# FNet mixing and a ReGLU feed-forward: feature tiles taken in pairs, two PSUM banks to one VectorE instruction

## The chip, the cores and the metric

The kernel runs on one core of one Trainium2 chip. The metric is the device time of one execution in microseconds. The kernel before takes 650.49 us, the median of three runs (649.2 to 650.72).

Engine names in the profile: PE is TensorE's matmul, PEld its weight load, DVE is VectorE, ACT is ScalarE, POOL is GpSimd, SP is the engine whose queue issues most transfers. PSUM is the memory in which these kernels place the tiles that PE writes; a tile of 128 x 512 fp32 in it is called a bank here. The granted clock is the share of its full clock that TensorE was given. L505 is line 505 of the kernel that the line belongs to. The two kernels have different line numbers.

## The reference

```python
# x: 8 x 3008 x 256, w_gate and w_val: 256 x 1536, w_out: 1536 x 256, all fp32
X = np.fft.fft(np.fft.fft(x, axis=1), axis=2).real      # FNet mixing
x = X.reshape(8 * 3008, 256)
gate = np.maximum(x @ w_gate, 0.0)
val = x @ w_val
out = (gate * val) @ w_out                               # 24064 x 256, fp32
```

## The kernel before

Each batch is transformed into tiles `pq` of 128 x 2 x 512 (bf16), three blocks of columns to a batch. The feed-forward then runs as 288 steps: 8 batches, 3 blocks, NF = 12 tiles of 128 features. The spectrum of a real input is symmetric, so one step serves 512 rows and their mirrored rows. With the two halves pq0 and pq1 and the weights wc, ws and wm (wm is -2 ws):

- gate: G = wc·pq0 + ws·pq1, and ScalarE takes its Relu, `gs`. Then G += wm·pq1 gives the mirrored gate, and ScalarE takes its Relu, `gm`.
- value: V = wc·pq0. VectorE makes E = nb·af + V from it (called the even below). Then V += ws·pq1, and VectorE takes the direct product h0 = gs·V.
- mirrored value: VectorE makes E = 2E - V (the reflection, L519), and GpSimd makes the mirrored product h1 = gm·E with its columns reversed (L511).
- unsplit (relief) steps skip the even and the reflection: PE makes the mirrored value by a third matmul, V += wm·pq1, and VectorE multiplies it (from step 216 on GpSimd does, from a copy that ScalarE makes). These are the first 18 steps, then every sixth up to step 48, then every twelfth.

The output matmuls of step t-12 (8 of 256 columns in each step) fill the gaps. GpSimd also folds the input rows of a later batch: `fold` is a generator, and the loop takes one piece from it in each step. The rows for it are asked for at step `tl` of a batch, and its first piece is emitted at step `tf`.

```python
def split(t):
    return 18 <= t < len(steps) and t % (6 if t < 48 else 12) != 5

def value(t, part):
    ...                                                  # cut
    if part == 0:
        e["V"] = psv.tile([128, 512], F32, tag="v", name="V")      # one bank, three of them
        nc.tensor.matmul(e["V"][:], lhsT=wc[1][:, fs], rhs=pq[:, 0, :], start=True, stop=split(t))
    else:
        nc.tensor.matmul(e["V"][:], lhsT=ws[1][:, fs], rhs=pq[:, 1, :], start=False, stop=True, ...)
        nc.vector.tensor_tensor(e["h"][:, 0, :], e["gs"][:], e["V"][:], op=ALU.mult)

def mirror_value(t):
    ...                                                  # cut
    if split(t):
        nc.vector.scalar_tensor_tensor(e["E"][:, cols], e["E"][:, cols], 2.0, e["V"][:, cols],
                                       op0=ALU.mult, op1=ALU.subtract)
        mirror_h(t, nc.gpsimd, e["E"])
    else:
        nc.tensor.matmul(e["V"][:, cols], lhsT=wm[1][...], rhs=pqt[b, blk][:, 1, cols], ...)
        ...                                              # cut

plan = {0: (18, 24, ...), 1: (7, 13, ...), 2: (7, 13, ...)}      # (tl, tf, steps of the transform)

for t in range(n + NF):
    if 0 < t <= n:
        mirror_gate(t - 1)
    if t < n:
        gate(t)
    if 0 < t <= n:
        if split(t - 1):
            value(t - 1, 1)
        else:
            mirror_value(t - 1)
    if t < n and not split(t):
        value(t, 0)
        value(t, 1)
    for fn in extra.get(t, ()):                          # loads, transform of the next batch
        fn()
    if t >= NF:
        out_piece(t - NF, 0)
    if split(t):
        value(t, 0)
        even(t)
    if t >= NF:
        out_piece(t - NF, 1)
    if 0 < t <= n and split(t - 1):
        mirror_value(t - 1)
    while folds and next(folds[0], folds) is folds:      # one piece of fold, at the end of the step
        folds.pop(0)
```

Of the kernel before, what the change touches and what calls it, by code (L numbers as in the profile page):

```python
# [43 lines left out]
def kernel(ctx: ExitStack, tc, x, w_gate, w_val, w_out, out):  # L44
# [12 lines left out]
    HB = 2 * NF + 1  # L57
# [5 lines left out]
    psd = ctx.enter_context(tc.tile_pool(name="psd", bufs=1, space=PS))  # L63
    psg = ctx.enter_context(tc.tile_pool(name="psg", bufs=2, space=PS))
    psv = ctx.enter_context(tc.tile_pool(name="psv", bufs=3, space=PS))
    pso = ctx.enter_context(tc.tile_pool(name="pso", bufs=2, space=PS))
# [76 lines left out]
    def bank(b, name):  # L143

        if b == 0:
            return psv.tile([128, 512], F32, tag="v", name=name)
        return psd.tile([128, 512], F32, tag="d", name=name)
# [3 lines left out]
    def stage1(b, c, evac):  # L151
# [4 lines left out]
        ps = bank(b, "ps1")  # L156
# [34 lines left out]
    def rotate(b):  # L191
        t4 = t4t[b]
        ps = bank(b, "psr")
        nc.tensor.matmul(ps[:, 0:NKA], lhsT=rot[:], rhs=t4[:, :, H], start=True, stop=True)
        nc.vector.tensor_copy(t4[:, :, H], ps[:, 0:NKA])
# [3 lines left out]
    def stage2(b, blk, cs, evac):  # L199
# [4 lines left out]
        ps = bank(b, "ps2")  # L204
        for g in range(4):
            nc.tensor.matmul(ps[:, g * 128:(g + 1) * 128], lhsT=t4[:, 4 * blk + g, cs * H:(cs + 1) * H],  # L206
                             rhs=m2[:, cs, :], start=True, stop=True)
        if evac == "act":
            nc.scalar.copy(pq[:, cs, :], ps[:])
        else:  # L210
            nc.vector.tensor_copy(pq[:, cs, :], ps[:])  # L211
# [26 lines left out]
    cd = None  # L238
    for n in range(DF // 512):
        if n == 2:  # L240
            cd = hp.tile([128, 2, H], F32, tag="h", name="cd")
        for i in range(2):
            for c in range(3):
                wst[i, n, c] = hp.tile([128, 512], F32, tag="h", name="wst")

    def load_w(n, which=(0, 1)):
        for i in which:
            w = (w_gate, w_val)[i]
            for c in range(2):
                nc.sync.dma_start(out=wst[i, n, c][:], in_=w[c * 128:(c + 1) * 128, n * 512:(n + 1) * 512])  # L250

    def pair_w(n, i, eng):

        lo, hi, up = (wst[i, n, c] for c in range(3))
        eng.tensor_tensor(up[:], lo[:], hi[:], op=ALU.add)
        eng.tensor_tensor(lo[:], lo[:], hi[:], op=ALU.subtract)

    def fold_w(n, i, cs, evac="act"):

        ps = (pso.tile([128, 512], F32, tag="o", name="psw") if i == 0 or n else  # L260
              psg.tile([128, 512], F32, tag="g", name="psw"))
        for k, w in ((0, wst[i, n, 2]), (1, wst[i, n, 0])):
            nc.tensor.matmul(ps[64 * k:64 * k + 64, :], lhsT=cd[:, cs, 64 * k:64 * k + 64], rhs=w[:],  # L263
                             start=True, stop=True)
# [8 lines left out]
    def nyquist():  # L273

        ps = psd.tile([128, 512], F32, tag="d", name="psn")
# [8 lines left out]
    with tc.tile_pool(name="sp", bufs=1, space=SB) as sp:  # L284
# [32 lines left out]
        ps = psd.tile([128, 512], F32, tag="d", name="psk")  # L317
# [67 lines left out]
        pl.iota(kbi[:], pattern=[[0, 4], [1, NB]], base=0, channel_multiplier=0, allow_small_or_imprecise_dtypes=True)  # L385
# [66 lines left out]
    ep = ctx.enter_context(tc.tile_pool(name="ep", bufs=4, space=SB))  # L452
# [3 lines left out]
    ht = {}  # L456

    def mirrored(t):

        blk = steps[t][1]  # L460
        return slice(NB if blk == 0 else 0, 512 - NB if blk == NBLK - 1 else 512)

    def split(t):

        return 18 <= t < len(steps) and t % (6 if t < 48 else 12) != 5

    def gate(t):
        b, blk, f = steps[t]
        pq, fs = pqt[b, blk], slice(f * 128, (f + 1) * 128)
        e = ht[t] = {"h": hp.tile([128, 2, 512], BF16, tag="h", name="h"),  # L470
                     "G": psg.tile([128, 512], F32, tag="g", name="G"),
                     "gs": gp.tile([128, 512], F32, tag="gs", name="gs")}
        nc.tensor.matmul(e["G"][:], lhsT=wc[0][:, fs], rhs=pq[:, 0, :], start=True, stop=False)  # L473
        nc.tensor.matmul(e["G"][:], lhsT=ws[0][:, fs], rhs=pq[:, 1, :], start=False, stop=True)  # L474
        nc.scalar.activation(e["gs"][:], e["G"][:], ACTF.Relu)  # L475
        cols = mirrored(t)
        if cols.stop - cols.start < 512:

            lo = 0 if cols.start else cols.stop
            nc.gpsimd.memset(e["h"][:, 1, lo:lo + NB], 0.0)  # L480

    def mirror_gate(t):
        b, blk, f = steps[t]
        e, cols = ht[t], mirrored(t)
        nc.tensor.matmul(e["G"][:, cols], lhsT=wm[0][:, f * 128:(f + 1) * 128], rhs=pqt[b, blk][:, 1, cols],  # L485
                         start=False, stop=True, skip_group_check=True)
        e["gm"] = ep.tile([128, 512], F32, tag="gm", name="gm")
        nc.scalar.activation(e["gm"][:, cols], e["G"][:, cols], ACTF.Relu)  # L488

    def value(t, part):  # L490
        b, blk, f = steps[t]
        e, pq, fs = ht[t], pqt[b, blk], slice(f * 128, (f + 1) * 128)
        if part == 0:
            e["V"] = psv.tile([128, 512], F32, tag="v", name="V")
            nc.tensor.matmul(e["V"][:], lhsT=wc[1][:, fs], rhs=pq[:, 0, :], start=True, stop=split(t))  # L495
        else:
            nc.tensor.matmul(e["V"][:], lhsT=ws[1][:, fs], rhs=pq[:, 1, :], start=False, stop=True,  # L497
                             skip_group_check=split(t))
            nc.vector.tensor_tensor(e["h"][:, 0, :], e["gs"][:], e["V"][:], op=ALU.mult)  # L499

    def even(t):
        b, blk, f = steps[t]
        e, cols = ht[t], mirrored(t)
        e["E"] = ep.tile([128, 512], F32, tag="e", name="E")
        nc.vector.scalar_tensor_tensor(e["E"][:, cols], nbt[b, blk][:, cols], af[:, f:f + 1], e["V"][:, cols],  # L505
                                       op0=ALU.mult, op1=ALU.add)

    def mirror_h(t, eng, val):

        e, cols = ht[t], mirrored(t)  # L510
        eng.tensor_tensor(free(e["h"][:], 512 + cols.start + NB - 1, [NB, (cols.stop - cols.start) // NB], [-1, NB]),  # L511
                          e["gm"][:, cols].rearrange("p (a k) -> p a k", k=NB),
                          val[:, cols].rearrange("p (a k) -> p a k", k=NB), op=ALU.mult)

    def mirror_value(t):
        b, blk, f = steps[t]
        e, cols = ht[t], mirrored(t)
        if split(t):
            nc.vector.scalar_tensor_tensor(e["E"][:, cols], e["E"][:, cols], 2.0, e["V"][:, cols],  # L519
                                           op0=ALU.mult, op1=ALU.subtract)  # L520
            mirror_h(t, nc.gpsimd, e["E"])
        else:
            nc.tensor.matmul(e["V"][:, cols], lhsT=wm[1][:, f * 128:(f + 1) * 128], rhs=pqt[b, blk][:, 1, cols],  # L523
                             start=False, stop=True, skip_group_check=True)
            if t < 6 * NBLK * NF:
                mirror_h(t, nc.vector, e["V"])
            else:
                e["E"] = ep.tile([128, 512], F32, tag="e", name="E")
                nc.scalar.copy(e["E"][:, cols], e["V"][:, cols])
                mirror_h(t, nc.gpsimd, e["E"])  # L530
# [3 lines left out]
    def out_piece(t, half):  # L534

        b, blk, f = steps[t]
        for k in range(8 * f + 4 * half, 8 * f + 4 * half + 4):
            gi, ff = divmod(k, NF)
            sg, s = divmod(gi, 4)
            g = 3 - s if sg else s  # L540
            if s == 0 and ff == 0:
                state["os"] = op.tile([128, 4, D], F32, tag="os", name="os")
            if s % 2 == 0 and ff == 0:
                state["po"] = pso.tile([128, 2, D], F32, tag="o", name="po")
            po, os_ = state["po"], state["os"]
            nc.tensor.matmul(po[:, s % 2, :], lhsT=ht[t - f + ff]["h"][:, sg, g * 128:(g + 1) * 128],  # L546
# [3 lines left out]
            if t - f == len(steps) - NF and sg == 1:  # L550
                nc.vector.tensor_copy(os_[:, s:s + 1, :], po[:, s % 2:s % 2 + 1, :])  # L551
                store_last(b, blk, os_, s)
                continue
            if s % 2 == 1:
                nc.scalar.copy(os_[:, s - 1:s + 1, :], po[:])  # L555
            if s == 3:
                store(b, blk, sg, os_)

    def store_last(b, blk, os_, s):

        for u in range(4):
            ka = NKA * u + 4 * blk
            if s == 0 and ka + 3 == 47:
                continue
            (nc.sync if u % 2 or s < 2 else nc.scalar).dma_start(
                out=view(out, (b * S + NA - ka - 3 + s) * D, [[NA * D, NB], [1, D]]), in_=os_[32 * u:32 * u + 32, s, :])

    def store(b, blk, sg, os_):
        for u in range(4):
            ka = NKA * u + 4 * blk  # L570
            src = os_[32 * u:32 * u + 32].rearrange("p g d -> p (g d)")
            if sg == 0:
                nc.sync.dma_start(out=view(out, (b * S + ka) * D, [[NA * D, NB], [1, 4 * D]]), in_=src)
                continue

            lo = 1 if ka + 3 == 47 else 0
            hi = 3 if ka == 0 else 4
            row = b * S + NA - ka - 3 + lo
            nc.sync.dma_start(out=view(out, row * D, [[NA * D, NB], [1, (hi - lo) * D]]),
                              in_=src[:, lo * D:hi * D])  # L580
# [89 lines left out]
```

## Time and profile before

| what | before | view |
|---|---|---|
| span of the profiled run | 648.3 us | page, head |
| PE busy from 300 to 400 us | 99% | windows |
| VectorE, GpSimd busy in the same stretch | 92%, 91% | windows |
| 36 steps (one batch) in the middle | 73.8 us | timeline, between gate Relus |
| GpSimd's waits for rows before `fold`, each batch | 1.4 to 3.0 us | timeline of GpSimd |

The page's first part has the busy time of each engine, as a share of the span, and the number of its instructions:

```profile
PE 626.1 (97%) x4170; PEld 408.8 (63%) x4246; DVE 565.0 (87%) x889; ACT 425.1 (66%) x813; POOL 508.1 (78%) x716
```

The windows view, for 300 to 400 us. After the length come the busy times of PE, PEld, DVE, ACT and POOL with their instructions, then the granted clock, the DMA share and GB/s:

```profile
300.00:400.00 100.00, 99.14 (x687) 66.52 (x699) 92.16 (x145) 68.59 (x132) 90.54 (x126) 1.00 0.45 111
```

PE has no gap worth a name in the middle of the kernel, at the full clock. VectorE and GpSimd are close behind it. Their times show in the timeline. Its columns are the start, the duration, the engine, the line, the operation, the tiles and their shapes; a bracket at the end, where there is one, gives the engine's idle time just before and who ended it. PE first, then VectorE in the same stretch:

```profile
311.97 0.38 PE L485 MATMUL G<-pq,wm 128*128 128x512 bf16 x1
312.19 0.38 PE L473 MATMUL G<-pq,wc 128*128 128x512 bf16 x1
312.40 0.38 PE L474 MATMUL G<-pq,ws 128*128 128x512 bf16 x1
```

```profile
311.15 0.69 DVE L499 TENSOR_TENSOR h<-gs,V 128x512 bf16<-128x512 f32 x1
311.81 0.75 DVE L505 SCALAR_TENSOR_TENSOR E<-nb,af,V 128x512 f32<-128x512 bf16 x1
312.47 0.68 DVE L519 SCALAR_TENSOR_TENSOR E<-E,V 128x512 f32<-128x512 f32 x1
313.11 0.69 DVE L499 TENSOR_TENSOR h<-gs,V 128x512 bf16<-128x512 f32 x1
```

A record of 0.38 us isn't PE's cost of a matmul: the next one starts 0.215 us later. VectorE's three instructions start 0.65 us apart and come round in 1.96 us.

### The profile page before, as it was taken

The page shows a single profiled execution, that of the slowest core. Times are in us where ns is not written, and L with a number is a line of the kernel's source. Part 1 is how long each engine was busy: PE and PEld are TensorE (multiplying, and loading weights), DVE is VectorE, ACT ScalarE, POOL GpSimd, SP SyncE. Part 2 cuts the span into 40 slices and gives each one's busy share as a digit, 9 for nine tenths or more (in the row PEclk, how much of TensorE's full clock was granted, in tenths as well). Part 3 has the DMA queues.
Part 4 walks back from the last instruction along what each step waited for, and adds up shares of the span by engine and source line. Part 5 has one row for each costly group of instructions (what it writes and reads, how often), then busy time and mean ns, then how long its engine had stood idle before and what let it go on. Part 6 is the DMA issues. An engine that isn't in the chain of part 4 may idle for free.

```text
span 648.3 us, 12804 instructions
## 1 busy us (share of the span) xinstructions
PE 626.1 (97%) x4170; PEld 408.8 (63%) x4246; DVE 565.0 (87%) x889; ACT 425.1 (66%) x813; POOL 508.1 (78%) x716
## 2 busy tenths in 40 slices
PE   7888999999999999999999999999999999999995
PEld 3424666666666666666666666666666666666664
DVE  8857688889898998989989998989988988989991
ACT  5465676776766667677676666676666766766660
POOL 9648669967998799968998699967998666666660
PEclk9699999999999999999999999999999999999999
DMA  9792483295125551195334752285312142112113
GB/s 234 241 234 46 104 215 85 69 208 168 40 82 120 143 161 45 47 199 146 81 74 115 165 148 55 50 177 152 96 50 73 31 131 73 50 34 64 32 41 88
DMA packets 32823, 70.77 MB, mean 109 GB/s; under 512 B 4650, under 2 KB 22146, under 8 KB 30754
## 3 DMA queue, kind: packets, MB, share of 16 engines
q1 hardware_dynamic: 30228, 58.03, 33.9%
q0 software_dynamic: 2336, 11.80, 8.7%
q8 instruction: 33, 0.54, 0.4%
q14 instruction: 34, 0.28, 0.1%
q10 hardware_dynamic: 192, 0.13, 0.1%
HBM read 39.77 MB, written 30.96 MB: 109 GB/s over the span
## 4 chain that ended last, share of the span: by engine, by line
PE 89%; DVE 6%; issue 2%; DMA 2%; ACT 1%; SPq 0%; DVEq 0%; ACTq 0%
PE po L546 38%; PE V L497 10%; PE G L474 9%; PE G L485 9%; PE V L495 8%; PE G L473 8%; PE ps L164 2%; PE ps L206 2%; DVE E L505 2%; DVE h L499 1%; PE V L523 1%; PE psw L263 1%; DMA xl<-in_x_dram 1%; DVE eo L136 1%; DVE eo L132 1%
## 5 line engine op out<-in xcount | busy, mean ns | idle before, releaser
L511 POOL TENSOR_TENSOR h<-gm,E 128x480 bf16<-128x480 f32 (+1 forms) x251 | 307.7, 1226 | 90.9 <-DVE E L519 63.9
L546 PE MATMUL po<-wo,h 128*128 128x256 bf16 x2304 | 337.1, 272 | 2.8 <-DVE os L551 1.1
L546 PEld LDWEIGHTS <-h 128*128 128x128 bf16 x2304 | 222.7, 98 | 91.1 <-issue 3.4
L488 ACT ACTIVATE gm<-G 128x480 f32<-128x480 f32 (+1 forms) x288 | 167.4, 581 | 126.8 <-PE G L485 118.7
L499 DVE TENSOR_TENSOR h<-gs,V 128x512 bf16<-128x512 f32 x288 | 195.7, 687 | 17.6 <-ACT gm L488 11.5
L505 DVE SCALAR_TENSOR_TENSOR E<-nb,af,V 128x480 f32<-128x480 bf16 (+1 forms) x245 | 177.6, 725 | 23.3 <-PE V L495 12.6
L475 ACT ACTIVATE gs<-G 128x512 f32<-128x512 f32 x288 | 171.8, 597 | 0.8 <-PE G L474 0.8
L519 DVE SCALAR_TENSOR_TENSOR E<-E,V 128x480 f32<-128x480 f32 (+1 forms) x245 | 161.2, 658 | 0.0
L497 PE MATMUL V<-pq,ws 128*128 128x512 bf16 x287 | 108.7, 379 | 2.2 <-DVE E L505 1.7
L485 PE MATMUL G<-pq,wm 128*128 128x480 bf16 (+1 forms) x288 | 106.7, 370 | 2.2 <-ACT gs L475 2.2
L474 PE MATMUL G<-pq,ws 128*128 128x512 bf16 x281 | 106.5, 379 | 2.2 <-DVE pq L211 0.4
L495 PE MATMUL V<-pq,wc 128*128 128x512 bf16 x255 | 96.6, 379 | 0.0
L473 PE MATMUL G<-pq,wc 128*128 128x512 bf16 x253 | 95.9, 379 | 0.1
L555 ACT COPY os<-po 128x512 f32<-128x512 f32 x94 | 55.0, 585 | 60.2 <-PE po L546 60.2
L104 POOL TENSOR_TENSOR eo<-xl 94x254 bf16<-94x254 f32 (+2 forms) x100 | 74.6, 750 | 0.4
L101 POOL TENSOR_TENSOR xl<-xl,xh 94x510 f32<-94x510 f32 (+2 forms) x50 | 65.9, 1319 | 3.9
L497 PEld LDWEIGHTS <-ws 128*128 128x128 bf16 x288 | 28.2, 98 | 33.7
L474 PEld LDWEIGHTS <-ws 128*128 128x128 bf16 x288 | 28.2, 98 | 31.5 <-issue 0.2
L511 DVE TENSOR_TENSOR h<-gm,V 128x480 bf16<-128x480 f32 (+1 forms) x37 | 24.6, 665 | 22.7 <-ACT gm L488 17.1
L174 ACT CAST t<-ps 96x512 bf16<-96x512 f32 x63 | 36.9, 586 | 5.7 <-PE ps L162 5.2
L495 PEld LDWEIGHTS <-wc 128*128 128x128 bf16 x288 | 28.1, 98 | 11.0 <-issue 4.3
L485 PEld LDWEIGHTS <-wm 128*128 128x128 bf16 x288 | 28.2, 98 | 7.6 <-issue 4.1
(108 smaller groups left out, 348.1 us busy)
## 6 DMA issues: line engine op xcount, KB each, us to landing
out_dram<-os SPq DMA_DIRECT2D x173, 128.0 KB
xl<-in_x_dram SPq DMA_DIRECT2D x7, 1360.0 KB
Td<-t SPq DMA_DIRECT2D x7, 768.0 KB
t<-Td SPq DMA_DIRECT2D x7, 768.0 KB
nb<-Nd SPq DMA_DIRECT2D x24, 128.0 KB
xl<-in_x_dram SPq DMA_DIRECT2D x7, 238.0 KB
xl<-in_x_dram SPq DMA_DIRECT2D x4, 384.0 KB
xh<-in_x_dram SPq DMA_DIRECT2D x4, 384.0 KB
```

The costliest lines, as they stand in the source:

```text
L473: nc.tensor.matmul(e["G"][:], lhsT=wc[0][:, fs], rhs=pq[:, 0, :], start=True, stop=False)
L474: nc.tensor.matmul(e["G"][:], lhsT=ws[0][:, fs], rhs=pq[:, 1, :], start=False, stop=True)
L475: nc.scalar.activation(e["gs"][:], e["G"][:], ACTF.Relu)
L485: nc.tensor.matmul(e["G"][:, cols], lhsT=wm[0][:, f * 128:(f + 1) * 128], rhs=pqt[b, blk][:, 1, cols], start=False, stop=True, skip_group_ ...
L488: nc.scalar.activation(e["gm"][:, cols], e["G"][:, cols], ACTF.Relu)
L495: nc.tensor.matmul(e["V"][:], lhsT=wc[1][:, fs], rhs=pq[:, 0, :], start=True, stop=split(t))
L497: nc.tensor.matmul(e["V"][:], lhsT=ws[1][:, fs], rhs=pq[:, 1, :], start=False, stop=True, skip_group_check=split(t))
L499: nc.vector.tensor_tensor(e["h"][:, 0, :], e["gs"][:], e["V"][:], op=ALU.mult)
L505: nc.vector.scalar_tensor_tensor(e["E"][:, cols], nbt[b, blk][:, cols], af[:, f:f + 1], e["V"][:, cols], op0=ALU.mult, op1=ALU.add)
L511: eng.tensor_tensor(free(e["h"][:], 512 + cols.start + NB - 1, [NB, (cols.stop - cols.start) // NB], [-1, NB]), e["gm"][:, cols].rearrange ...
L519: nc.vector.scalar_tensor_tensor(e["E"][:, cols], e["E"][:, cols], 2.0, e["V"][:, cols], op0=ALU.mult, op1=ALU.subtract)
L546: nc.tensor.matmul(po[:, s % 2, :], lhsT=ht[t - f + ff]["h"][:, sg, g * 128:(g + 1) * 128], rhs=wo[:, ff, :], start=(ff == 0), stop=(ff == ...
```

## The change

The intent: VectorE pays its fixed cost (about 0.11 us an instruction by the prediction's estimate) once for two steps, so that it no longer needs the relief steps and their extra matmul. Steps run in pairs. The pair's V, E, gs, gm and h are tiles of two banks or two halves; product and reflection cover both in one instruction; the two evens stay single. PSUM is divided anew: two V pairs of two banks (before: three single banks), no bank kept for the transform, which borrows the output bank that is idle. The column blocks shift by 16, so that the mirrored part is 496 or 512 columns wide and the direct one 496, 512 or 497. VectorE's copy of the rotation goes to ScalarE. Some pieces of the next batch's transform move by one or two steps in the plan. E and gm have three pair buffers (before: four single ones).

The core of the diff. The new output code, the row lists for the stores, the banks of the first transform and the removed lines of the old loop are cut.

```diff
-    psd = ctx.enter_context(tc.tile_pool(name="psd", bufs=1, space=PS))
-    psv = ctx.enter_context(tc.tile_pool(name="psv", bufs=3, space=PS))
-    pso = ctx.enter_context(tc.tile_pool(name="pso", bufs=2, space=PS))
+    psv = ctx.enter_context(tc.tile_pool(name="psv", bufs=2, space=PS))
+    pso = ctx.enter_context(tc.tile_pool(name="pso", bufs=1, space=PS))
...
+    def borrow(name):
+        return pso.tile([128, 512], F32, tag=f"o{(turn['o'] + 1) % 2}", name=name)
...
-    ep = ctx.enter_context(tc.tile_pool(name="ep", bufs=4, space=SB))
+    ep = ctx.enter_context(tc.tile_pool(name="ep", bufs=3, space=SB))
...
     def split(t):
-        return 18 <= t < len(steps) and t % (6 if t < 48 else 12) != 5
+        return t >= NF
...
+    def direct_h(p):
+        t = 2 * p
+        ds = direct(t)
+        nc.vector.tensor_tensor(pair(t, "h")[:, :, 0, 0:ds.stop - ds.start], pair(t, "gs")[:, :, ds],
+                                pair(t, "V")[:, :, ds], op=ALU.mult)
...
+            nc.vector.scalar_tensor_tensor(E[:, :, cols], E[:, :, cols], 2.0, V[:, :, cols],
                                            op0=ALU.mult, op1=ALU.subtract)
+            mirror_h(p, nc.gpsimd, E)
...
+    def between(t):
         for fn in extra.get(t, ()):
             fn()
         while folds and next(folds[0], folds) is folds:
             folds.pop(0)
+    for p in range(n + NF // 2):
+        t = 2 * p
+        live = p < n
+        if 0 < p <= n:
+            mirror_gate(t - 1)
+        if live:
+            gate(t)
+            value(t, 0)
+            if not split(t):
+                value(t, 1)
+        fill(t, 0)
+        between(t)
+        if live:
+            value(t + 1, 0)
+            if not split(t):
+                value(t + 1, 1)
+        if 0 < p <= n:
+            (direct_h if split(t - 1) else mirror_value)(p - 1)
+        if live:
+            if split(t):
+                even(t)
+                even(t + 1)
+        fill(t, 1)
+        if live:
+            mirror_gate(t)
+            gate(t + 1)
+            if not split(t):
+                direct_h(p)
+        fill(t + 1, 0)
+        between(t + 1)
+        if 0 < p <= n and split(t - 1):
+            mirror_value(p - 1)
+        if live:
+            for k in range(2):
+                value(t + k, 1 if split(t) else 2)
+        fill(t + 1, 1)
```

## The prediction

> What bounds it now. From step 48 on, TensorE. The windows of 200 to 500 us show PE busy 99%, and a batch of 36 steps, read in the timeline between the gate's first Relus (step 72 at 190.14 us, step 108 at 263.90), takes 73.8 us. The timeline spaces 512-column matmuls by 215 ns, 480 by 202, 256 by 108; 36 steps of about 4587 columns, three relief matmuls and the next batch's transform add up to the same 73.8. So PE has no gap there. VectorE is as full in unrelieved steps: its three instructions start 0.65 us apart, 1.94 us per step, PE's step too. The page's 687 ns includes a tail that overlaps the next start; the fixed part is about 0.11 us.
>
> What changes from step 12 on.
> - PE: direct blocks shrink to 496/512/497 columns, mirrored ones go from 480/512/480 to 496/512/496: about 31 columns, 13 ns, less per step: 276 steps, 3.5 us.
> - The 31 relief steps lose their 202-215 ns matmul: 6.4 us.
> - VectorE per pair: product 1003/0.96+0.11 = 1.16 us, reflection 1.16, two evens 1.27: 3.6 us against PE's 3.86. It was 3.9. Slack, no time by itself.
> - GpSimd: about 2.3 us per pair instead of 2.4; 192 memsets of 0.12 us vanish.
> - ScalarE takes the rotation: small.
> So a steady batch should be 72.7 us; steps 36 to 72 gain 3.7, 12 to 36 2.6, the last batch 1.6 us. In the tail, two PE waits of 0.5 us on the last output copies go, as each group has its own bank. About 15 us in all.
>
> What it costs.
> - The first 12 steps are unsplit. Today they overlap step by step (26.1 us between the Relus of steps 0 and 12). In pairs they become a loop: second gate, ScalarE's two Relus (0.45 us apart), one product of 1.2 us over both banks, then the mirrored value matmuls, the next pair. I add up 4.5 us per pair without weight folding against 3.05 now; folds and copies in even steps lie in the chain too: about 33 us. Cost 7 us.
> - The fold of batch 2 (three-row pieces, about 1.35 us per step) with 1.15 us of reflections gives GpSimd 2.5 us per step against PE's 2.0, from step 24 to 41. Without relief it falls behind by 5-7 us; the three E buffers cover about 3. Cost 2-3 us, once.
> - Output blocks of 112 or 113 columns: [...] The trace agrees that 96-column loads are slower, 123 ns against 98, though matmuls behind them kept 108 ns spacing. 384 such matmuls; I count 0-2 us.
>
> Sum: 650.5 - 15 + 7 + 2.5 + 1 = 646; I think some head losses overstated and say 644 us, range 635 to 652. Chances: faster over 2% 0.13, within 2% 0.83, slower 0.04. The gain is capped because the relieved engine was tied with PE, not above it.
>
> Signs. Right: 36 steps at 72.7 us in the middle; VectorE waiting on PE at its evens; no third value matmul after step 12; steps 0 to 12 about 33 us, with PE waiting on VectorE's product. Wrong: middle batches of 74 us or more, PE waiting on VectorE, on ScalarE's output copy (borrowed bank) or on GpSimd; or a head of 26 us.
>
> What would make it wrong: two-bank VectorE reads slower per column than one-bank ones; 112-column loads not hidden (up to 5 us); GpSimd's lag stalling every batch; a head better overlapped than I think (then 637).

650.5 - 15 + 7 + 2.5 + 1 comes to 646, from which the prediction goes to 644. The 1 us for the narrower output blocks is an estimate: in the trace before, the 105 loads of 96 columns of L164 have a mean of 124 ns, those of 128 columns one of 98.

## More of the kernel before

L99 is the first instruction of a piece of `fold`, and it waits for the rows to land, six times in all, for 11.5 us. Here is one such wait, with the issue of the load on SP's queue and then GpSimd's timeline:

```profile
277.87 0.82 SPq L83 DMA_DIRECT2D xl<-in_x_dram  x2
```

```profile
295.97 0.22 POOL L99 TENSOR_TENSOR eo<-xl,xh 94x4 bf16<-94x4 f32 x1 [1.92 <-DMA xh<-in_x_dram,ix]
...
297.49 1.27 POOL L511 TENSOR_TENSOR h<-gm,E 128x512 bf16<-128x512 f32 x1
```

The fold goes on 18.1 us after SP asked for the rows. What it waited for last are the rows of `xh`, which GpSimd had asked for itself at 277.49 us. GpSimd stands still for 1.92 us, then mixes pieces of `fold` and mirrored products, and nobody waits for it long enough to hold up PE.

The summary of waits gives, for each pair of waiting line and releaser, the total, the count and the longest. Two lines of GpSimd's:

```profile
POOL eo L99 <- DMA xh<-in_x_dram,ix: 9.3, 5, 3.0
POOL eo L99 <- DMA xl<-in_x_dram: 2.2, 1, 2.2
```

## The result, and the profile after

| | median of runs | lowest to highest | runs |
|---|---|---|---|
| before, same rounds | 650.61 us | 649.2 to 651.59 | 4 |
| after | 691.69 us | 689.94 to 693.12 | 4 |

The ratio is 1.0632, with a 95% interval of 1.0598 to 1.0666: the change costs 6.3%. Ratios here are the mean time of one kernel's runs over the mean of the other's of the same rounds, so they aren't quite the ratio of the medians quoted beside them. The result is correct. It lies far outside the predicted range of 635 to 652 us.

Where the 42.9 us between the two profiled spans came from, read in the timeline from the start of the gate's first Relu at each step:

| stretch | before | after | difference | predicted |
|---|---|---|---|---|
| start, to step 0 | 35.51 | 38.51 | +3.0 | 0 |
| steps 0 to 12 | 26.11 | 34.90 | +8.8 | +7 |
| steps 12 to 36 | 52.15 | 56.99 | +4.8 | -2.6 |
| steps 36 to 72 | 76.37 | 81.53 | +5.2 | -3.7 + 2.5 |
| steps 72 to 216, four batches with a fold | 295.90 | 313.79 | +17.9 | -1.1 each |
| steps 216 to 252, a batch without a fold | 73.84 | 74.76 | +0.9 | -1.1 |
| steps 252 to 276 | 47.62 | 49.23 | +1.6 | about -1.1 |
| step 276 to the end | 40.8 | 41.5 | +0.7 | about -1.5 |

The table already holds a hint. There are eight batches, and rows are folded two batches ahead, so the seventh (from step 216) has no fold in it. It takes 74.76 us where the four before it take 78.4 on average. So two things are wrong in the steady part: about 3.7 us a batch that come with the fold, and about 2 us a batch, against the predicted 72.7, that don't.

The page after, its first part and GpSimd's row of busy tenths in 40 slices:

```profile
PE 636.6 (92%) x4200; PEld 414.0 (60%) x4231; DVE 548.6 (79%) x630; ACT 432.7 (63%) x846; POOL 512.6 (74%) x412
...
POOL 9539458995999589975999579974999555555552
```

VectorE's instructions went from 889 to 630 and its busy time fell by 16 us, as intended. It bought nothing: PE's share fell from 97% to 92%. GpSimd is busy 74% in all, but its row swings between 4 or 5 tenths and 9 in a steady beat, one swing for each batch. The windows view of 300 to 400 us shows the same loss; PE was at 99.14 there:

```profile
300.00:400.00 100.00, 96.02 (x656) 64.61 (x660) 83.84 (x94) 68.77 (x136) 75.93 (x60) 1.00 0.52 124
```

The waits after (the line numbers are those of the new kernel: L98 is the old L99, L538 the old L511, L525 the even, L546 the reflection, L518 the value matmuls, L531 the direct product):

```profile
DVE E L525 <- PE V L518: 47.7, 82, 2.6
DVE E L525 <- POOL h L538: 42.3, 32, 4.1
POOL eo L98 <- DMA xl<-in_x_dram: 26.4, 4, 7.0
POOL eo L98 <- DMA xh<-in_x_dram,ix: 23.4, 3, 10.5
...
PE V L518 <- DVE E L525: 22.0, 18, 3.7
...
PE V L518 <- DVE h L531: 10.5, 6, 2.5
```

Of the waits for rows, 10.5 us are one wait in the start, which is not new: the traces of the kernel before and of its two variants below have it too, at 10.6 to 11.1 us. Read from the bottom up, these lines are a chain. PE waits for VectorE's evens; the evens wait for GpSimd's mirrored products; and GpSimd waits for rows. One instance, in the order of cause. SP asks for the rows, and GpSimd waits for them:

```profile
305.47 0.78 SPq L82 DMA_DIRECT2D xl<-in_x_dram  x2
```

```profile
323.04 0.22 POOL L98 TENSOR_TENSOR eo<-xl,xh 94x4 bf16<-94x4 f32 x1 [6.55 <-DMA xl<-in_x_dram]
323.33 1.26 POOL L100 TENSOR_TENSOR xl<-xl,xh 94x510 f32<-94x510 f32 x1
324.56 2.27 POOL L538 TENSOR_TENSOR h<-gm,E 128x992 bf16<-128x992 f32 x1
```

```profile
316.98 1.18 DVE L546 SCALAR_TENSOR_TENSOR E<-E,V 128x992 f32<-128x992 f32 x1
...
326.87 1.41 DVE L525 SCALAR_TENSOR_TENSOR E<-nb,af,V 128x512 f32<-128x512 bf16 x2 [3.40 <-POOL h L538]
```

```profile
328.33 0.59 PE L518 MATMUL V<-pq,ws 128*128 128x512 bf16 x2 [2.44 <-DVE E L525]
```

The reflection that the mirrored product at 324.56 reads was ready at 316.98 + 1.18 = 318.16 us. The product ran 6.4 us later, because the piece of `fold` stood ahead of it in GpSimd's queue and waited for rows. So GpSimd took the two in the order of the program here: a product that was ready waited behind a piece that wasn't. That is what "in order" means below. The rows (a load of 1360 KB, one of 238 KB and an indirect one) were there 17.6 us after they were asked for, much as before (18.1), so the load isn't slower. What changed is the place in the queue. In the loop before, the first piece at step 13 stands behind the mirrored product of step 12. In the new loop it stands ahead of the one for steps 10 and 11. The wait grew from 1.92 to 6.55 us.

The second thing shows in a stretch without transform and fold. One pair of steps, from the mirrored gate of one pair to that of the next:

```profile
603.34 0.37 PE L510 MATMUL G<-pq,wm 128*128 128x496 bf16 x1
...
605.89 0.60 PE L570 MATMUL po<-wo,h 128*128 128x256 bf16 x4
606.52 0.58 PE L518 MATMUL V<-pq,ws 128*128 128x496 bf16 x2
606.93 0.60 PE L570 MATMUL po<-wo,h 128*128 128x256 bf16 x4
607.37 0.37 PE L510 MATMUL G<-pq,wm 128*128 128x496 bf16 x1
```

The pair takes 4.03 us. Four output matmuls last 0.44 us (606.93 to 607.37), so those at 605.89 end at about 606.33, and the two value matmuls start 0.2 us late. (Where a transform gives PE other work, part of this is hidden: a batch of 18 pairs loses 1.9 us to it, as product_late shows below.) VectorE in another such pair:

```profile
629.72 1.41 DVE L525 SCALAR_TENSOR_TENSOR E<-nb,af,V 128x512 f32<-128x512 bf16 x2 [0.48 <-PE V L518]
631.04 1.21 DVE L546 SCALAR_TENSOR_TENSOR E<-E,V 128x1024 f32<-128x1024 f32 x1
632.17 1.21 DVE L531 TENSOR_TENSOR h<-gs,V 128x1024 bf16<-128x1024 f32 x1
```

VectorE sits idle for 0.48 us before its evens, although the first bank of V was written more than half a microsecond before the second (603.97 and 604.61 us in the pair above). The waits that the built program carries say why (not from the profile; a listing of VectorE's instructions and of what each waits for):

```
L546 E<-E,V    [waits DVE]
L531 h<-gs,V   [waits PE, Activation]
L525 E<-nb,af,V   [waits PE, Pool]
L525 E<-nb,af,V
```

The first even carries the wait for PE, the second carries none: both wait until both banks are written. The value matmuls behind them likewise wait for both evens. The pair's tile is one unit to the bookkeeping of waits.

The third thing is the head, which the prediction named. VectorE and PE after:

```profile
42.26 1.19 DVE L531 TENSOR_TENSOR h<-gs,V 128x992 bf16<-128x992 f32 x1 [1.70 <-ACT gs L505]
```

```profile
43.51 0.58 PE L518 MATMUL V<-pq,wm 128*128 128x496 bf16 x2 [2.53 <-DVE h L531]
...
44.68 0.62 PE L504 MATMUL G<-pq,ws 128*128 128x496 bf16 x1
45.09 0.62 PE L518 MATMUL V<-pq,wc 128*128 128x496 bf16 x1
```

PE waits 2.53 us for the one product over both banks. Its matmuls then last 0.62 us and start 0.41 us apart, from 44.0 to 47.4 us; the granted clock of 43.5 to 46 us is 0.60, that of 44.0 to 47.4 us 0.50.

### The profile page after: what moved, and what is told of

It reads as the page before. It is cut to its first block, busy times and chain, and to the rows that moved or that the text cites. A ratio compares the mean times of both kernels' runs of the same rounds, so it can differ in the third digit from the quotient of the medians.

```text
span 691.2 us, 11747 instructions
## 1 busy us (share of the span) xinstructions
PE 636.6 (92%) x4200; PEld 414.0 (60%) x4231; DVE 548.6 (79%) x630; ACT 432.7 (63%) x846; POOL 512.6 (74%) x412
## 4 chain that ended last, share of the span: by engine, by line
PE 46%; POOL 24%; DMA 13%; DVE 7%; issue 5%; ACT 2%; SPq 1%; POOLq 0%; DVEq 0%; ACTq 0%
PE po L570 19%; PE V L518 12%; POOL h L538 10%; DMA xl<-in_x_dram 7%; POOL xl L100 5%; DMA xh<-in_x_dram,ix 5%; POOL eo L103 5%; DVE E L525 4%; PE G L504 4%; PE G L510 4%; PE G L503 4%; POOL eo L131 2%; PE psw L274 1%; DVE h L531 1%; SPq L621 1%
## 5 line engine op out<-in xcount | busy, mean ns | idle before, releaser
L538 POOL TENSOR_TENSOR h<-gm,E 128x992 bf16<-128x992 f32 (+1 forms) x138 | 319.6, 2316 | 99.5 <-DVE E L546 99.5
L570 PE MATMUL po<-wo,h 128*128 128x256 bf16 (+2 forms) x2304 | 343.5, 273 | 0.6
L570 PEld LDWEIGHTS <-h 128*128 128x128 bf16 (+2 forms) x2304 | 233.9, 103 | 122.0 <-issue 1.8
L525 DVE SCALAR_TENSOR_TENSOR E<-nb,af,V 128x496 f32<-128x496 bf16 (+1 forms) x276 | 191.0, 734 | 101.6 <-PE V L518 47.7
L512 ACT ACTIVATE gm<-G 128x496 f32<-128x496 f32 (+1 forms) x288 | 170.3, 591 | 154.3 <-PE G L510 131.3
L531 DVE TENSOR_TENSOR h<-gs,V 128x992 bf16<-128x992 f32 (+2 forms) x144 | 172.0, 1194 | 6.1 <-ACT gs L505 5.1
L505 ACT ACTIVATE gs<-G 128x497 f32<-128x497 f32 (+2 forms) x288 | 169.4, 588 | 1.4 <-PE G L504 1.4
L546 DVE SCALAR_TENSOR_TENSOR E<-E,V 128x992 f32<-128x992 f32 (+1 forms) x138 | 164.4, 1192 | 0.0
L518 PE MATMUL V<-pq,wc 128*128 128x497 bf16 (+2 forms) x288 | 109.0, 378 | 0.0
L510 PE MATMUL G<-pq,wm 128*128 128x496 bf16 (+1 forms) x288 | 108.9, 378 | 0.0
L518 PE MATMUL V<-pq,ws 128*128 128x496 bf16 (+2 forms) x276 | 83.9, 378 | 24.8 <-DVE E L525 22.0
L518 PEld LDWEIGHTS <-ws 128*128 128x128 bf16 x288 | 27.4, 97 | 42.1 <-issue 39.6
L504 PEld LDWEIGHTS <-ws 128*128 128x128 bf16 x288 | 28.4, 99 | 33.3 <-issue 1.3
L98 POOL TENSOR_TENSOR eo<-xl,xh 94x4 bf16<-94x4 f32 (+2 forms) x50 | 10.9, 219 | 49.8 <-DMA xl<-in_x_dram 26.4
L518 PEld LDWEIGHTS <-wc 128*128 128x128 bf16 x288 | 28.4, 99 | 21.4 <-issue 4.1
```

The costliest lines, as they stand in the source:

```text
L504: nc.tensor.matmul(G[:, ds], lhsT=ws[0][:, fs], rhs=pq[:, 1, ds], start=False, stop=True)
L505: nc.scalar.activation(pair(t, "gs")[:, t % 2, ds], G[:, ds], ACTF.Relu)
L510: nc.tensor.matmul(G[:, cols], lhsT=wm[0][:, f * 128:(f + 1) * 128], rhs=pqt[b, blk][:, 1, cols], start=False, stop=True, skip_group_check ...
L512: nc.scalar.activation(pair(t, "gm")[:, t % 2, cols], G[:, cols], ACTF.Relu)
L518: nc.tensor.matmul(pair(t, "V")[:, t % 2, cs], lhsT=w[:, f * 128:(f + 1) * 128], rhs=pqt[b, blk][:, min(k, 1), cs], start=(k == 0), stop=( ...
L525: nc.vector.scalar_tensor_tensor(pair(t, "E")[:, t % 2, cols], nbt[b, blk][:, cols], af[:, f:f + 1], pair(t, "V")[:, t % 2, cols], op0=ALU ...
```

## The experiments

Theory A: GpSimd's queue is blocked by a piece of `fold` whose rows haven't landed, because it was moved ahead of the mirrored product; the stall passes through the three E buffers to VectorE and PE. Its rival: GpSimd has too much to do, with no relief, whatever the order; and another rival, that the pairs themselves are slow. Theory C: the steady pair is slow because a tile of two banks is waited for as one. Its rival: a two-bank read on VectorE costs more per column, or the output blocks of 112 columns load slowly. Theory D: the head is the loop that the prediction described.

All times by stretch, in us, from the gate Relus of the profiled runs:

| kernel | to step 0 | 0-12 | 12-36 | 36-72 | 72-108 | 108-144 | 216-252 | 252-276 | median of runs |
|---|---|---|---|---|---|---|---|---|---|
| before | 35.51 | 26.11 | 52.15 | 76.37 | 73.76 | 73.84 | 73.84 | 47.62 | 650.61 |
| after | 38.51 | 34.90 | 56.99 | 81.53 | 78.42 | 78.31 | 74.76 | 49.23 | 691.69 |
| late_fold | 39.22 | 33.31 | 50.75 | 78.94 | 74.76 | 75.11 | 74.75 | 49.22 | 669.70 |
| product_late | 38.38 | 33.31 | 54.82 | 81.29 | 78.59 | 78.77 | 72.89 | 46.64 | 684.43 |
| head_overlap | 37.83 | 25.74 | 58.13 | 81.68 | 78.81 | 78.33 | 74.75 | 49.23 | 684.61 |
| late_and_product | 38.37 | 34.85 | 49.21 | 78.14 | 73.43 | 72.99 | 72.84 | 46.63 | 655.41 |
| load_early | 38.17 | 36.07 | 51.13 | 86.28 | 74.76 | 75.12 | 74.77 | 49.23 | 676.24 |
| even_order | 38.37 | 33.31 | 60.69 | 86.12 | 84.10 | 83.28 | 82.78 | 54.31 | 736.14 |
| before_fold_early | 37.45 | 26.11 | 55.76 | 82.23 | 80.96 | 81.09 | 73.85 | 47.62 | 690.96 |
| all_mended | 36.49 | 25.74 | 50.37 | 77.89 | 73.42 | 73.00 | 72.84 | 46.65 | 645.27 |
| spread_fold | 36.89 | 25.74 | 50.38 | 79.43 | 77.76 | 75.44 | 72.83 | 46.65 | 664.22 |
| before_late | 35.94 | 26.11 | 52.15 | 75.86 | 73.63 | 73.84 | 73.85 | 47.62 | 650.03 |

The first twelve steps vary from 33.3 to 36.1 us among six kernels that have the same loop there, each profiled once. The clock accounts for part of it. A wait of 2.53 us ends at 43.4 to 44.2 us in late_fold, even_order, late_and_product and the change. In the first two the matmuls behind it go on 0.21 us apart, and the stretch takes 33.31 us, as in product_late. In the other two they start 0.41 us apart, until 47.4 us in the change and 46.6 us in late_and_product, and the stretch takes 34.90 and 34.85 us. What decides between the two outcomes is not shown here. Differences of that size in that column are not read below. The start varies too, from 35.51 to 37.45 us among the three kernels with the old start.

### late_fold: the fold starts when its rows are there

The new kernel with one number changed in each line of the plan.

```diff
-    plan = {0: (18, 24, ...), 1: (7, 13, ...), 2: (7, 13, ...)}
+    plan = {0: (18, 28, ...), 1: (7, 16, ...), 2: (7, 16, ...)}
```

> The change, with the folds' start moved from step 13 (24 for the first) to step 16 (28) and nothing else. Theory A (GpSimd's queue is blocked by a fold piece whose input rows have not landed, and the reflections wait behind it): the 5.6 to 7.3 us waits of the fold on the loads shrink to under 2, VectorE's waits on GpSimd (42 us in the change) fall below 15, time about 668 us (660 to 674). Rival B (GpSimd simply has more work than fits): the work is the same, so VectorE's waits move three steps but stay, time 685 to 692.

Measured: 669.7 us, ratio to before 1.030 (1.0283 to 1.0318). That is 22.0 us less than the change as it came. The waits:

```profile
POOL eo L98 <- DMA xh<-in_x_dram,ix: 10.5, 1, 10.5
...
DVE E L525 <- POOL h L538: 6.2, 5, 1.8
```

Of seven waits for rows two are left: the one in the start, and one of 1.2 us in the second batch. The evens' wait for GpSimd fell from 42.3 to 6.2 us. Batches with a fold now take 74.8 to 75.1 us, as the one without. GpSimd does exactly the same work, so the rival "too much work" falls for the steady batches; it stands for steps 36 to 72, where 78.94 us remain. No run put the piece back behind the mirrored product and left its step unchanged, so how much of the 22.0 us the order within the step makes, and how much the start ahead of the rows, is not measured apart.

### load_early: the same cure from the other side

Here the fold stays early and the rows are asked for earlier.

```diff
-    plan = {0: (18, 24, ...), 1: (7, 13, ...), 2: (7, 13, ...)}
+    plan = {0: (14, 24, ...), 1: (4, 13, ...), 2: (4, 13, ...)}
```

> The change, with the load of the next rows asked for three steps earlier (step 4 instead of 7, 14 instead of 18 in the first batch) and the fold left where it is. Theory A says that what blocks GpSimd is the landing of the rows, so this should do as well as the late fold did: waits of the fold on the loads under 2 us each (the first, of 10.5 us at the very start, stays), time about 670 us (666 to 676). If it is the fold's place in the queue that costs and not the missing data, the time stays at 688 to 692.

Measured: 676.24 us, 1.0386 (1.0366 to 1.0406). All batches from step 72 on agree with late_fold to 0.02 us. So it's the landing of the rows against the start of the fold, not the fold's place in the batch as such. It came out worse than late_fold for one reason that I had not foreseen: in the second batch, GpSimd waited once more for 6.43 us, and steps 36 to 72 took 86.28 us. The load for that batch writes the buffer that the fold issued in the first batch is still reading. The last instruction of that fold ended at 142.59 us; SP's queue started the load at 142.62, although its step had come some 8 us earlier, and the rows landed 18.0 us later. One such wait made that stretch 7.3 us longer than in late_fold.

### before_fold_early: the disease given to the kernel before

If what matters is that the fold reaches GpSimd's queue before its rows are there, and the pairs are innocent, then the kernel before, with single banks and its relief steps, must fall ill from an earlier fold alone.

```diff
-    plan = {0: (18, 24, ...), 1: (7, 13, ...), 2: (7, 13, ...)}
+    plan = {0: (18, 21, ...), 1: (7, 10, ...), 2: (7, 10, ...)}
```

> The kernel before, with the fold started three steps earlier (10 instead of 13, 21 instead of 24). Theory A: it gets the same disease, since its rows land 16 steps into the batch: waits of the fold on the loads grow from about 2 us to 6 to 8 us per batch, four E buffers of one step cover some 3 us, so TensorE loses 2 to 4 us in each of six batches and the time is about 666 us (659 to 674). Rival B (only pairs suffer, by their size or GpSimd load): 650 to 653 us.

Measured: 690.96 us, 1.0619 (1.06 to 1.0638), as slow as the change itself, from one number in each line. The sign was right, and the size was a miss: I had expected 666 us. The trace shows why. GpSimd's stall, and PE around it:

```profile
314.37 0.22 POOL L99 TENSOR_TENSOR eo<-xl,xh 94x4 bf16<-94x4 f32 x1 [7.90 <-DMA xh<-in_x_dram,ix]
```

```profile
317.98 0.58 PE L497 MATMUL V<-pq,ws 128*128 128x512 bf16 x1 [4.93 <-DVE E L505]
...
320.49 0.63 PE L485 MATMUL G<-pq,wm 128*128 128x512 bf16 x1
320.92 0.63 PE L473 MATMUL G<-pq,wc 128*128 128x512 bf16 x1
```

After a wait of 4.93 us, PE's matmuls of 512 columns start 0.43 us apart where 0.215 is normal. The windows view gives a granted clock of 0.50 for 318.0 to 322.2 us; from 322.95 us on, matmuls of 512 columns start 0.21 to 0.22 us apart again. So the stall is paid twice: as the wait, and then as about 4.2 us at half speed, worth another 2.1 by that count. In the head of the changed kernel the clock was halved after a wait of 2.53 us (above); after another of 2.44 us, at 328.33, it was not (1.00 from 328 to 333 us). How long a wait must be for this is not shown here.

### before_late: the counter-check

The cure of late_fold in the kernel before.

```diff
-    plan = {0: (18, 24, ...), 1: (7, 13, ...), 2: (7, 13, ...)}
+    plan = {0: (18, 27, ...), 1: (7, 16, ...), 2: (7, 16, ...)}
```

> The kernel before, with its folds three steps later (16 instead of 13, 27 instead of 24), as the mended kernel has them. It waits only 1.4 to 3 us per batch for the rows and four E buffers cover that, so nothing to gain: 648 to 651 us. It shows whether the mended kernel's gain over the kernel before is the pairs' or only the later fold's.

Measured: 650.03 us against 650.16, 0.9996 (0.9982 to 1.0009). GpSimd's small waits of each batch are gone but for one of 1.4 us, and the time is the same. So in the kernel before the folds started late enough, its waits of 1.4 to 3.0 us cost nothing that can be measured, and what a mended version gains over it does not come from a later fold.

### product_late and late_and_product: one unit for two banks

The value matmuls that wait for the two evens move behind four more output matmuls, so that the whole pair of evens is done when PE gets to them.

```diff
-        if live:
+        if live and not split(t):
             for k in range(2):
-                value(t + k, 1 if split(t) else 2)
+                value(t + k, 2)
         fill(t + 1, 1)
+        if live and split(t):
+            for k in range(2):
+                value(t + k, 1)
```

Alone:

> The change, with the second pair of value matmuls moved behind the last four output matmuls of the pair; same instructions. Theory C (both evens start only when the second value bank has been written, so they end 0.2 us after TensorE wants to add to the banks): the gap of about 0.2 us per pair before these matmuls goes, a pair without transform takes 3.85 us instead of 4.05 to 4.1, time about 673 us (666 to 681). If the pairs stay at 4.05 and the wait reappears at another place, VectorE's chain itself is the limit and the time stays at 688 to 692.

Measured: 684.43 us, 1.0519 (1.05 to 1.0538). The batch without a fold falls from 74.76 to 72.89 us, and steps 252 to 276 from 49.23 to 46.64. The batches with a fold stay at 78.3 to 78.8. This was a miss in the sum: 1.9 us a batch should come with every batch, but where GpSimd sets the pace, a faster pair on PE only waits longer. And the clock was no better: the mean granted clock of the profiled run is 0.973, where the change's is 0.976. Together with late_fold:

> Both of the first two edits. If A and C are separate causes the savings add: about 650 us (643 to 658). With pairs of 3.85 us GpSimd has 2.25 us of reflection and about 1.9 us of fold in each pair of a fold window, more than fits, so I expect some VectorE waits on GpSimd to stay there (10 to 20 us in all).

Measured: 655.41 us, 1.0065 (1.0034 to 1.0096). On top of late_fold the same edit is now worth 14.3 us, where alone it was worth 7.3; the other way round, late_fold's edit is worth 29.0 us on top of this one, where alone it was worth 22.0. I had expected VectorE to wait 10 to 20 us for GpSimd still; it waits 8.7 us. PE in a pair:

```profile
566.52 0.37 PE L510 MATMUL G<-pq,wm 128*128 128x496 bf16 x1
...
567.15 1.04 PE L570 MATMUL po<-wo,h 128*128 128x256 bf16 x8
568.02 0.58 PE L518 MATMUL V<-pq,ws 128*128 128x496 bf16 x2
...
570.36 0.37 PE L510 MATMUL G<-pq,wm 128*128 128x496 bf16 x1
```

The pair takes 3.84 us and has no gap: eight output matmuls (0.87 us) end where the value matmuls start. Steady batches take 72.84 us; 72.7 was predicted. So the prediction's sum of columns was right, and the rivals of C fall: VectorE's records and the loads of 112 columns are the same in this kernel, and its batches are not slow. Those loads do take 131 ns where 128 columns take 98 (in the changed kernel; 130 here):

```profile
L570 PEld LDWEIGHTS <-h 128*112 128x112 bf16 x288 | 34.6, 131 | 11.8 <-issue 0.5
```

But the loads run while other matmuls do (in the changed kernel PEld is busy 60% of the span and PE 92%), and the four matmuls behind them keep their 0.43 us (561.53 to 561.96 us there).

### even_order: is it the tile that is waited for?

If the two banks were tracked one by one, the order "first bank, its even, second bank, its even" would let VectorE start earlier. If the tile is the unit, the second bank's matmul must now wait for the first even, which reads another bank.

```diff
         fill(t, 0)
+        if 0 < p <= n and split(t - 1):
+            direct_h(p - 1)
+        if live and split(t) and split(t - 1):
+            even(t)
         between(t)
         if live:
             value(t + 1, 0)
             if not split(t):
                 value(t + 1, 1)
-        if 0 < p <= n:
-            (direct_h if split(t - 1) else mirror_value)(p - 1)
-        if live:
-            if split(t):
+        if 0 < p <= n and not split(t - 1):
+            mirror_value(p - 1)
+        if live and split(t):
+            if not split(t - 1):
                 even(t)
-                even(t + 1)
+            even(t + 1)
```

> The change, with the product of the pair before and the first even written into the program ahead of the second value matmul, so that the first even no longer waits for that matmul. Same instructions, same order on VectorE. If the two banks of a pair count as one tile, the second bank's matmul now waits for VectorE's reading of the first: the gap moves from the reflected value matmuls to the second value matmul and the time stays within 1% of the change (686 to 700). If the banks were told apart, the 0.2 us per pair would go: about 673 us.

Measured: 736.14 us, 1.1313 (1.1292 to 1.1334). The waits, and one instance on VectorE and PE:

```profile
PE V L518 <- DVE E L525: 65.4, 138, 4.0
```

```profile
627.14 0.73 DVE L525 SCALAR_TENSOR_TENSOR E<-nb,af,V 128x496 f32<-128x496 bf16 x1
628.33 0.73 DVE L525 SCALAR_TENSOR_TENSOR E<-nb,af,V 128x496 f32<-128x496 bf16 x1 [0.46 <-PE V L518]
```

```profile
627.92 0.37 PE L518 MATMUL V<-pq,wc 128*128 128x497 bf16 x1 [0.46 <-DVE E L525]
```

The wait occurs 138 times, and there are 138 split pairs. PE's write to the second bank is held up by VectorE's read of the first, by 0.46 us in the instance above, and the second even then waits for PE in turn. This shows the unit. The size was larger than I expected (686 to 700 us): 12 steps (240 to 252) take 27.4 us, 4.57 a pair; the likely reason is that PE and VectorE now take turns with each other twice in every pair. The waits that this program carries guard the two banks together, and this run shows what that costs.

### head_overlap: the loop of the first twelve steps

The mirrored value matmuls of an unsplit pair are issued one pair later, behind the next pair's gate.

```diff
         if 0 < p <= n:
+            if not split(t - 1):
+                value(t - 2, 2)
+                value(t - 1, 2)
             (direct_h if split(t - 1) else mirror_value)(p - 1)
...
-        if live:
+        if live and split(t):
             for k in range(2):
-                value(t + k, 1 if split(t) else 2)
+                value(t + k, 1)
```

> The change, with the mirrored value matmuls of each of the first six pairs moved behind the next pair's first value matmuls, so that TensorE has work while VectorE multiplies. Theory D (in the first 12 steps the loop second gate, two Relus, one product over both banks, value matmuls is serial): step 0 to step 12 falls from 34.9 us to 28 to 31, time about 686 us (684 to 689). If it stays at 34, the folding and ScalarE limit the start, not the product.

Measured: 684.61 us, 1.0519 (1.0502 to 1.0537), 7.1 us less than the change. Steps 0 to 12 take 25.74 us, against 34.90 and, before, 26.11; the clock granted from 38 to 50 us is 1.00, where it was 0.86. So the head's loss was the loop, as theory D says: 7.2 us by the traces in which the clock held (33.31 against 26.11). The halved clock, which theory D did not have, added 1.6 us in the change's trace.

### all_mended: the parts together

late_fold, product_late, head_overlap, and a change to the banks of the first transform, which alternate between the first half of a new pair tile and a spare output bank, so that no two of them share a tile.

```diff
     def early(name):
-        if turn["v"] % 2 == 0:
-            turn["t"] = psv.tile([128, 2, 512], F32, tag="v", name=name)
         turn["v"] += 1
-        return turn["t"][:, (turn["v"] - 1) % 2, :]
+        if turn["v"] % 2 == 0:
+            return spare(name)
+        return psv.tile([128, 2, 512], F32, tag="v", name=name)[:, 0, :]
```

> Late fold, late product and overlapped head together, and in the first transform and rotation one bank per tile instead of halves of a pair. From the run with the first two (655.4 us): minus 7 for the head as measured alone, minus about 3 for the start (first Relu at 38.4 us back to 35.5), gives 645 us (641 to 649), which would beat the kernel before by about 1%. Left over: the fold of batch 2, which overloads GpSimd around step 36 to 48 (about 4 us).

Measured: 645.27 us, the median of six runs (644.85 to 646.14), against 650.33: 0.992 (0.9907 to 0.9934). It beats both kernels, the one before by 0.8%, which is a real difference. Its page:

```profile
PE 617.5 (96%) x4231; PEld 409.7 (64%) x4231; DVE 551.8 (86%) x630; ACT 433.3 (67%) x846; POOL 512.4 (80%) x412
```

PE's busy time is at least 8.6 us less than before (617.5 against 626.1, and some of the matmul records of the kernel before are missing): the pairs do save what they were made to save. The first gate comes at 36.49 us (36.89 in spread_fold, which has the same start); the seven traces with the changed kernel's start have it between 37.83 and 39.22. The change to the banks was never run alone, so what it is worth, and the rest of the start's delay, is not settled.

### spread_fold: the last stretch

all_mended still takes 77.89 us for steps 36 to 72. The fold that begins at step 28 takes rows three at a time, and its 17 pieces reach into this second batch. Theory: GpSimd has too much work there. Here those pieces are cut to two rows, and all loads and folds are moved later.

```diff
-        xc = XC if b < 3 else 2
+        xc = XC if b < 2 else 2
...
-    plan = {0: (18, 28, ...), 1: (7, 16, ...), 2: (7, 16, ...)}
+    plan = {0: (15, 24, ...), 1: (14, 23, ...), 2: (13, 22, ...)}
```

> The mended kernel, with the fold of batch 2 cut into pieces of two rows instead of three (26 pieces over 26 steps, 0.94 us per step on GpSimd instead of 17 pieces of 1.35 us per step), and the loads and folds of all batches moved later together (fold from step 24, 23 or 22 of the batch, its load 9 steps earlier). If the 4.5 us still lost between steps 36 and 48 (28.8 us against 24.2 in later batches) come from GpSimd having more work than fits there, they go and the time is 641 us (639 to 643). If the loss has another source in the first batch, it stays at 645.

Measured: 664.22 us, 1.0227 (1.02 to 1.0253), a miss. The part that it was made for came true: steps 36 to 48 fell from 28.81 to 24.73 us, so the fold in three-row pieces from step 28 cost 4.1 us more there than the one in two-row pieces from step 24. But later in each batch a new wait appeared:

```profile
PE psr L205 <- DMA t<-Td: 16.2, 5, 4.3
```

The load of the rows now runs at the same time as the shuffle of the transform through DRAM, whose data PE needs for the rotation: in one batch the rows are asked for at 296.67 us and the shuffle begins at 308.66. Its way out takes 9.3 us there, where the same batch of all_mended, with the load 25 us ahead, takes 4.4. PE waits for them five times, 16.2 us in all. A time for the loads that is clear of both was not looked for.

## Why the prediction was wrong

The result of 691.69 us lies outside the range of 635 to 652, on the side to which the prediction gave 0.04.

What held, point by point:

- "From step 48 on, TensorE" is the bound before. The windows show 99%, and before_late shows that GpSimd's waits cost it nothing.
- The count of PE's columns. A steady batch without false waits takes 72.84 us; 72.7 was predicted.
- VectorE's two-bank instructions: 1.16 us was estimated, with 0.96 columns a ns. The trace before bears that out: its reflections of 480 and 512 columns take 647 and 680 ns, 33 ns for 32 columns; the trace after has 1214 ns for 1024, 534 more for 512 more. The 0.65 us from start to start, less 0.534 for 512 columns, leaves about 0.12 us of fixed cost; 0.11 was estimated. In the trace after, the reflection at 631.04 is followed by the next start 1.13 us later. VectorE waits on PE at its evens, as foretold.
- The head: about 33 us predicted with PE waiting for the product, 34.90 measured. The loop was right (33.31 us in the traces in which the clock held). What it missed is the clock, halved after the first wait of 2.53 us in this trace (0.50 from 44.0 to 47.4 us).
- 112-column loads: 0 to 2 us predicted, none seen.

What failed were two steps.

First, "Cost 2-3 us, once", said of GpSimd and the fold. This step counted GpSimd's work per step in the second batch, and that term was fair: the fold in three-row pieces cost 4.1 us there by spread_fold. But it asked only how much GpSimd has to do, not in which order. The change moved the piece of `fold` ahead of the mirrored product in an in-order queue, and its rows land about 17.6 us after they are asked for, later than the queue reaches it. The last line of the prediction names "GpSimd's lag stalling every batch" as a risk, yet the 9.3 and 2.2 us of waits for rows that show it were in the profile before, in plain view, and weren't used. late_fold measures the cost: 22.0 us, or 29.0 once the product is late. before_fold_early shows that a fold ahead of its rows does it in the old loop, without any pair. Part of the cost is the clock: after the start, the change's trace has 13.7 us at half clock (0.50 from 44.0 to 47.4, 112.3 to 119.0 and 484.4 to 487.7 us) and the one before has none until its end (1.00 from 28 to 644 us), which is at most 6.8 us of the 42.9, 1.6 of them in the head.

Second, "Slack, no time by itself", and "So a steady batch should be 72.7 us". The prediction summed each engine's busy time over a pair, 3.6 us for VectorE against 3.86 for PE, and took the difference for slack. It did not draw the ring: both banks of V written, both evens, then both value matmuls. With one tile for two banks, each handover waits for the slower half, and PE stands still 0.2 us in each pair that no transform fills. product_late, once the fold is out of the way, measures 14.3 us for it, and even_order shows the unit directly.

Smaller terms: the head cost 8.8 us against 7, 7.2 without the clock; the start cost 3.0 us in these two profiles that were not foreseen, and how much of that is the change is open, as the old start alone varies by 1.9; the gain in the tail was not seen. The three cures, 22.0 + 14.3 + 7.1 = 43.4 us, lead from 691.69 to 648.3; with the banks of the start as well, all_mended measures 645.27. It keeps the pairs and the freed banks, and differs from the changed kernel only in the order of its instructions, the steps at which folds start and the banks of the first transform: those cost 46 us. Its 645.27 stands near the 644 predicted partly by luck: its steady batches gain 1.0 us each as foreseen, but steps 36 to 72 lose 1.5 us against the kernel before, where a net gain of 1.2 was predicted, and the head does not lose 7.

What found the causes here was to follow the waits back: PE's gaps, then VectorE's wait, then GpSimd's, then the DMA.

## What to carry to other kernels

When a change reorders what an engine is given that works in order, as GpSimd did here, ask of each instruction that waits for a transfer what stands behind it in the queue, and whether the data is there by then; a wait that costs nothing today is the margin that tells how far it may move. When two buffers become one tile, draw the ring of handovers again: each now waits for the slower half, and an engine that was slack in the sum can be late in the ring; putting other work between producer and consumer gets it back. A busy share doesn't name the engine that sets the pace: GpSimd, held up in its queue, was busy 76% in the window of 300 to 400 us, less than PE's 96% and VectorE's 84%. And a stall on TensorE can cost more than its length: behind waits of 2.53 and 4.93 us here, matmuls started 0.41 and 0.43 us apart instead of 0.21.
